# A conditioned attention and mixer block on one core: value products in one burst a unit, spread low halves in the MLP, attention's transfers in source order

## The chip, the core and the metric

The kernel runs on one core of a Trainium2 chip. The core has a matrix engine (TensorE, "PE" in the profile, with its weight loads shown apart as "PEld"), VectorE (DVE), ScalarE (ACT), GpSimdE (POOL) and SyncE (SP), which issues most of the transfers between memory (DRAM) and the on-chip buffers. Each engine works through its own queue in order and waits on semaphores for the others. TensorE writes its results to PSUM, which has eight banks; the other engines take them from there. The metric is the device time of one execution in microseconds (us).

## The reference

A sequence of 2048 rows of width 576 goes through attention over a sliding window of 256 rows, with 32 heads of 18, and then through a mixer block; both are modulated by a condition vector:

```
mod = silu(c) @ w_mod                      # sa, ca, ga, sb, cb, gb: six vectors of 576
h = layernorm(x) * (1 + ca) + sa
x = x + ga * (attention(h @ wqkv) @ wo)    # row i sees rows i-255 .. i
h = layernorm(x) * (1 + cb) + sb
x1 = h + shift(gelu(layernorm(h) @ w1)) @ w2       # quarters of the width shifted by +1, -1, +2, -2 rows
B  = x1 + gelu(layernorm(x1) @ w3) @ w4            # the MLP, hidden width 4608
x = x + gb * B
```

All data is float32. Large products are made in three parts: each operand is split into a high half (rounded to the engine's fast float32 form) and a low half (what is left), and high x high, high x low and low x high are added up.

## The kernel before

The kernel has three stages. The order of the work is written as a list of (time, function) pairs, which `play` sorts by time and runs; so a "time" in the code is a place in the order, not a duration. Under `manual_schedule` the engines named there keep that order; the queues of engines not named are ordered by the compiler's scheduler. In the attention stage and in the MLP, TensorE, VectorE, ScalarE and GpSimdE keep the written order, and SyncE's transfers are placed by the scheduler.

**Attention (phase_a).** Time counts units: 32 units, one for four heads of one group of 512 rows. For unit u, `pack(u)` at u-1.6 brings the unit's queries and keys by twelve transfers (L467, L469) into one of three buffers Q, K. Between u-1 and u, sixteen score products (L483) each go to VectorE for a masked maximum (L490). The maxima are transposed (L504), copied by ScalarE into a small tile `ms` (L509) and put by a transfer of ScalarE's queue (L510) into two more rows of the queries. Then, from u+0.38, the scores are made again, transposed, with the maximum already subtracted (L530, and L539 for the mask); ScalarE turns them into exponentials in tiles P (L549). A third of a unit has four heads in two P tiles; there are three thirds, b = 0, 1, 2. `av(b)` (L560) multiplies P with the values V: 32 columns of TensorE for each head. The results are copied to `avs` (L565), transposed (L571), divided and stored (L581). Between these, TensorE makes the queries, keys and values of the next group (L391), whose results pass POOL's split (L416) and are stored (L428 to L434), and later the output product with Wo (L785, stage s4). The raw weights wr of wqkv come through 'P' and 'r' buffers.

**Mixer (phase_b).** Products with w1 (L1016) and w2 (L1067). It isn't changed.

**MLP (phase_c).** Two blocks of 1024 rows, 18 units of 256 hidden columns each. `up` of a unit makes four wide results (L1276, 56 matmuls of 512 columns), which go through gelu on ScalarE to tiles g. From four g, POOL makes three combinations (L1249), so that the second product takes seven parts, m = 1, 2, 7, 4, 5, 6, 3 (a Strassen scheme). Each part is split: ScalarE writes the high half of a tile G (L1241), VectorE the low half (L1244). `down` of the unit before makes the seven narrow runs of twelve matmuls of 288 columns (L1322), into one of three pairs of PSUM banks; VectorE adds each pair of results to accA or accB (L1331). TensorE alternates: half of a wide result, a narrow run, and so on. In the first block the weights are also prepared: w3 and w4 are loaded (w4's rows are the tiles r, L1143), r is scaled by VectorE (L1164), combined by POOL (L1173), split by ScalarE and POOL (L1153, L1158; L1188, L1192), and the split weights are stored to w3d (L1160) and w4d (L1193). The second block only loads them again.

Of the kernel before, what the change touches and what calls it, by code (L numbers as in the profile page):

```python
# [18 lines left out]
D = 576  # L19
F = 4608  # L20
P = 128
# [32 lines left out]
class Kern:  # L54
# [134 lines left out]
    def phase_a(self):  # L189
# [9 lines left out]
        with ExitStack() as st:  # L199
# [91 lines left out]
            def w_load(c):  # L291
                def f():
                    raw = kp.tile([P, 1024], F32, tag="P", name=f"wr{c}", bufs=4)[:, 0:640] if c in (0, 4, 5, 1) else row(f"wr{c}")
# [178 lines left out]
            def scores(u):  # L472
# [34 lines left out]
                def ms():  # L507
                    ms = kp.tile([8, 512], F32R, tag="ms", name=f"ms{u}", bufs=1)
# [6 lines left out]
                return e + [(u + 0.01, neg), (u + 0.1, mt), (u + 0.115, ms)]  # L515
# [4 lines left out]
            def attend(u):  # L520
# [62 lines left out]
                for b in range(3):  # L583
# [3 lines left out]
                    e.append((u + self.o_x + (b + 1) / 3 + self.o_a, av(b)))  # L587
# [38 lines left out]

            def wo_begin():
                Wo["w"] = self.wv("Wo")
                Wo["ga"] = row("ga")[:, 0:D]
                nc.sync.dma_start(Wo["ga"], self.modd[2].to_broadcast([P, D]))  # L630

            def s4_begin():
                rows = gp.tile([P, 8, D], F32, tag="L", name="s4rows", bufs=1)
                self.s4row = lambda name: rows[:, next(cnt) % 8]
                self.sb, self.cb = (kp.tile([P, 1024], F32, tag="qe", name=n, bufs=2)[:, 0:D] for n in ("sb", "cb"))
                nc.sync.dma_start(self.sb, self.modd[3].to_broadcast([P, D]))
                nc.sync.dma_start(self.cb, self.modd[4].to_broadcast([P, D]))

            def wo_one(k, t):
                def f():  # L640
                    raw = row(f"wor{k}")[:, 0:D]
                    if k < KC:
                        nc.sync.dma_start(raw, self.wo[k * P:(k + 1) * P, :])
                        h, l = Wo["w"][:, k, :], Wo["w"][:, KC + k, :]
                    else:
                        self.load_dup(raw, self.wo[KC * P:, :])
                        h, l = Wo["w"][:, 2 * KC, :], Wo["w"][:, 2 * KC + 1, :]
                    Wo[k] = raw, h, l

                def scale():  # L650
                    raw = Wo[k][0]
                    nc.gpsimd.tensor_tensor(out=raw, in0=raw, in1=Wo["ga"], op=ALU.mult)

                def hi():
                    nc.scalar.copy(Wo[k][1], Wo[k][0])

                def lo():
                    raw, h, l = Wo[k]
                    nc.vector.tensor_tensor(out=l, in0=raw, in1=h.bitcast(F32), op=ALU.subtract)
                return [(t, f), (t + 0.2, scale), (t + 0.3, hi), (t + 0.36, lo)]  # L660
# [753 lines left out]
```

## Time and profile before

| | |
|---|---|
| median of 3 runs | 1755.18 us (1754.0 to 1764.7) |
| profiled execution | 1758.84 us |
| its span, first to last instruction | 1756.4 us |
| mean granted clock of TensorE | 0.990 |
| TensorE busy | 1684.1 us, 96% |
| VectorE busy | 1154.6 us, 66% |
| GpSimdE busy | 816.2 us, 46% |
| ScalarE busy | 711.8 us, 41% |

Times of one execution are read from the profile, whose own execution took 1758.84 us; the comparison of two kernels goes by the runs. A row of a group gives the line, the engine, the tiles written and read, the shape and the count; then busy time, the mean of one in ns, and the idle time before it with what ended most of it. A row of waits gives who waited for whom: us in all, how often, and the longest. A row of the timeline gives start and length in us, the engine and line, and in brackets the idle time before it. A row of a stretch gives its length, each engine's busy time, and then TensorE's granted clock, the share of the transfer engines, and GB/s. Attention fills the span up to some 690 us, the mixer up to some 860, the MLP the rest.

### The profile page before, as it was taken

The numbers are of one execution on the slowest core, as the hardware profiler recorded it, in microseconds if no ns is written. First come the engines' busy times: TensorE is split into PE (matmuls) and PEld (weight loads), VectorE is DVE, ScalarE is ACT, GpSimd is POOL, SyncE is SP. The second block draws the span as 40 slices with busy tenths as digits, with TensorE's granted clock in tenths as the row PEclk, the third lists the DMA queues.
The fourth block names the chain that finished last, engine by engine and source line by source line (L and its number), as shares of the span: only waits on it lengthen the run. The fifth ranks groups of instructions, "written<-read, shape, count | busy, mean of one in ns | idle before, by whom it ended". The sixth has DMA issues, their size and how long they took to land.

```text
span 1756.4 us, 30862 instructions
## 1 busy us (share of the span) xinstructions
PE 1684.1 (96%) x11100; PEld 1434.2 (82%) x11100; DVE 1154.6 (66%) x2543; ACT 711.8 (41%) x1310; POOL 816.2 (46%) x799
## 2 busy tenths in 40 slices
PE   8899999999999998999999999999999999999998
PEld 6767677777867776888988888888888999999997
DVE  3465565665667774767776666766676666666667
ACT  3254454554556556443344344434432222222321
POOL 7333141332235552134378777878865333333324
PEclk9999999999999999999999999999999999999999
DMA  6554445444356663545355555555555544444442
GB/s 196 175 164 144 117 140 143 129 132 128 98 151 189 198 197 124 180 126 169 129 207 177 171 203 206 183 176 201 202 212 195 161 149 153 147 150 158 154 142 74
DMA packets 161279, 283.33 MB, mean 161 GB/s; under 512 B 38500, under 2 KB 77412, under 8 KB 161128
## 3 DMA queue, kind: packets, MB, share of 16 engines
q1 hardware_dynamic: 158184, 275.54, 49.4%
q10 hardware_dynamic: 2944, 5.83, 1.2%
q8 instruction: 88, 1.44, 0.3%
q14 instruction: 63, 0.52, 0.1%
HBM read 168.86 MB, written 111.78 MB: 160 GB/s over the span
## 4 chain that ended last, share of the span: by engine, by line
PE 66%; POOL 9%; DVE 9%; DMA 7%; issue 4%; SPq 2%; ACT 2%; ACTq 0%; DVEq 0%; POOLq 0%
PE pall L1276 16%; PE pall L1322 16%; PE pall L391 8%; PE pall L560 4%; PE pall L530 4%; PE pall L483 4%; PE pall L1016 3%; PE pall L539 2%; PE pall L1067 2%; PE pall L785 2%; POOL g L1249 2%; POOL c L1173 2%; DMA r<-in_B_w_dram 2%; DVE accA L1331 1%; POOL W L1158 1%
## 5 line engine op out<-in xcount | busy, mean ns | idle before, releaser
L1276 PE MATMUL pall<-LNT,W 128*128 128x512 f32 x2016 | 501.1, 391 | 0.0
L1322 PE MATMUL pall<-W,G 128*128 128x288 f32 x3036 | 449.9, 296 | 20.8 <-DVE accB L1331 12.0
L1322 PEld LDWEIGHTS pall<-W,G 128*128 128x128 f32 x3036 | 431.5, 189 | 45.8 <-DVE accB L1331 16.3
L1276 PEld LDWEIGHTS pall<-LNT,W 128*128 128x128 f32 x2016 | 367.4, 189 | 60.5
L490 DVE CUSTOM_DVE_ANT_0 pall<-pall,mask 128x384 f32<-128x384 f32 (+2 forms) x512 | 271.8, 542 | 197.1 <-PE pall L483 194.4
L1331 DVE TENSOR_TENSOR accA<-pall,accA 128x576 f32<-128x576 f32 x336 | 248.4, 753 | 127.5 <-PE pall L1322 120.7
L1249 POOL TENSOR_TENSOR g<-g,g 128x512 f32<-128x512 f32 x140 | 191.1, 1365 | 257.1 <-ACT g L1280 240.6
L549 ACT ACTIVATE P<-pall 128x512 f32<-128x512 f32 (+2 forms) x384 | 216.5, 571 | 221.8 <-PE pall L539 199.9
L1244 DVE TENSOR_TENSOR G<-g,G 128x512 fp32r<-128x512 f32 x249 | 227.0, 928 | 50.0 <-ACT G L1241 49.8
L1241 ACT CAST G<-g 128x512 fp32r<-128x512 f32 x249 | 154.9, 622 | 239.9 <-POOL g L1249 236.4
L1280 ACT ACTIVATE g<-pall 128x512 f32<-128x512 f32 x144 | 85.8, 596 | 321.7 <-PE pall L1276 316.0
L483 PE MATMUL pall<-K,Q 108*128 108x384 f32 (+2 forms) x512 | 191.0, 380 | 10.1 <-DMA k1d<-qe 4.4
L530 PE MATMUL pall<-Q,K 110*128 110x384 f32 (+1 forms) x704 | 156.4, 296 | 10.0 <-ACT P L549 7.3
L391 PE MATMUL pall<-hT,Wc 128*128 128x512 f32 x504 | 160.2, 416 | 1.3 <-ACT V L454 1.0
L530 PEld LDWEIGHTS pall<-Q,K 110*128 110x128 f32 x704 | 123.7, 191 | 35.9 <-ACT P L549 16.1
L1331 DVE TENSOR_TENSOR accB<-pall,accB 128x576 f32<-128x576 f32 x134 | 97.8, 750 | 65.8 <-PE pall L1322 64.8
L416 POOL CAST qe<-qe 128x512 fp32r<-128x512 f32 x36 | 22.7, 630 | 253.2 <-ACT qe L412 233.1
L539 PE MATMUL pall<-maskb,identb 128*128 128x256 bf16 (+1 forms) x640 | 121.0, 255 | 0.0
L483 PEld LDWEIGHTS pall<-K,Q 108*128 108x128 f32 x512 | 97.5, 193 | 22.3 <-issue 11.4
L560 PE MATMUL pall<-P,V 128*32 128x384 f32 (+2 forms) x1408 | 100.5, 396 | 0.0
L391 PEld LDWEIGHTS pall<-hT,Wc 128*128 128x128 f32 x504 | 86.9, 194 | 13.7 <-issue 4.1
L391 PE MATMUL pall<-Wv,hT 128*128 128x288 f32 x448 | 84.1, 311 | 2.6 <-POOL Wv L334 2.4
(648 smaller groups left out, 2067.7 us busy)
## 6 DMA issues: line engine op xcount, KB each, us to landing
w4d<-W SPq DMA_DIRECT2D x55, 576.0 KB
W<-w4d SPq DMA_DIRECT2D x55, 576.0 KB
w3d<-W SPq DMA_DIRECT2D x36, 640.0 KB
W<-w3d SPq DMA_DIRECT2D x36, 640.0 KB
K<-k0d SPq DMA_DIRECT2D x96, 108.0 KB
r<-in_B_w_dram SPq DMA_DIRECT2D x36, 288.0 KB
Q<-q0d SPq DMA_DIRECT2D x128, 72.0 KB
K<-k1d SPq DMA_DIRECT2D x48, 108.0 KB
```

What stands on the lines that cost most here:

```text
L391: nc.tensor.matmul(pm, pl()[i][0], pl()[i][1], start=(i == 0), stop=(i == 13))
L483: nc.tensor.matmul(sc[:, lo:], q[0:2 * R3, h, i * P:(i + 1) * P], k[0:2 * R3, h // 2, i * P + lo:(i + 3) * P], start=True, stop=True)
L490: nc.vector.tensor_tensor_reduce(out=sc[:, lo:], in0=sc[:, lo:], in1=mask[:, lo:], scale=1.0, scalar=-3e38, op0=ALU.add, op1=ALU.max, accu ...
L530: nc.tensor.matmul(x[:, p0 * P:(p0 + w) * P], k[0:2 * R3 + 2, h // 2, (kb + 2) * P:(kb + 3) * P], q[0:2 * R3 + 2, h, q0 * P:(q0 + w) * P], ...
L539: nc.tensor.matmul(x[:, p0 * P:(p0 + w) * P], self.identb, m, start=False, stop=(n == len(ms) - 1))
L549: nc.scalar.activation(pt[:, c0:c1, h % 2, :], x[:, c0 * P:c1 * P].rearrange("p (a b) -> p a b", b=P), AF.Exp, scale=SCALE)
L560: nc.tensor.matmul(abox[0][32 * h:32 * h + 32, q0 * P:(q0 + w) * P], v[:, hh * VA:hh * VA + 32], Pt[b, h // 2][:, p0:p0 + w, h % 2, :], st ...
L1244: nc.vector.tensor_tensor(out=sp[m][:, 1], in0=src(), in1=sp[m][:, 0].bitcast(F32), op=sub)
L1249: nc.gpsimd.tensor_tensor(out=g[o] if o in g else gt(o), in0=g[a], in1=g[b], op=op)
L1276: nc.tensor.matmul(box["p"], box["l"][i][1], box["l"][i][0], start=(i == 0), stop=(i == 13))
L1322: nc.tensor.matmul(po, a, b, start=(n == 0), stop=(n == len(seq) - 1))
L1331: nc.vector.tensor_tensor(out=acc2[m, i], in0=po, in1=acc2[m, i], op=ALU.add)
```

## The change

It changes the order of the work and some buffers; every product, split and transfer is still made. Its parts:

1. The three `av(b)` of a unit stand directly behind one another at the end of the unit. Seven P tiles instead of four; `ms` uses the buffer of `avs`; a reserved scratch space is made smaller, which gives the room. The transposes of the maxima come 0.03 unit later.
2. In phase_a SyncE is under the written order as well. Some places move: the raw weights wr6 earlier, `pack(1)` from -0.6 to -1.5, the loads of Wo earlier and its splits farther behind them, sb and cb later, x rows of s4 earlier.
3. In the MLP the splits of G are spread over the unit, one low half behind each narrow run; two of POOL's combinations write to other tiles; scaling and combining of r come about 0.15 unit later; the stores to w3d and w4d are events of their own (`keep`), 0.3 unit behind the high halves.
4. The last unit of the first block runs its parts in the common order, with its final sums and stores to match.

```
-                            Pt[b, h // 2] = kp.tile([P, 4, 2, P], F32, tag="P", name=f"P{u}_{b}_{h}", bufs=4)
+                            Pt[b, h // 2] = kp.tile([P, 4, 2, P], F32, tag="P", name=f"P{u}_{b}_{h}", bufs=7)
...
-                    ms = kp.tile([8, 512], F32R, tag="ms", name=f"ms{u}", bufs=1)
+                    ms = kp.tile([8, 512], F32R, tag="avs", name=f"ms{u}", bufs=1)
...
-                return e + [(u + 0.01, neg), (u + 0.1, mt), (u + 0.115, ms)]
+                return e + [(u + 0.01, neg), (u + 0.13, mt), (u + 0.15, ms)]
...
-                    e.append((u + self.o_x + (b + 1) / 3 + self.o_a, av(b)))
+                    e.append((u + self.o_x + 1 + self.o_a - 0.001 * (2 - b), av(b)))
...
-            wt = {0: -8.975, 4: -8.974, 5: -8.973, 1: -8.972, 6: -2.7, 2: -1.9, 7: -1.5, 3: -1.2, 8: -0.9}
+            wt = {0: -8.975, 4: -8.974, 5: -8.973, 1: -8.972, 6: -7.45, 2: -1.9, 7: -1.5, 3: -1.2, 8: -0.9}
...
-                ev.append((u - self.o_p if u else -7.3, pack(u)))
+                ev.append((u - self.o_p if u > 1 else (-7.3, -1.5)[u], pack(u)))
...
-            ev += [(w1 - 1.25, wo_begin), (w1 + 0.03, s4_begin)]
+            ev += [(w1 - 1.7, wo_ga), (w1 - 1.15, wo_begin), (w1 + 0.03, s4_begin), (w1 + 0.4, s4_mod)]
             for k in range(KC + 1):
-                ev += wo_one(k, w1 - 1.2 + 0.12 * k)
+                ev += wo_one(k, w1 - 1.65 + 0.1 * k)
...
-            with self.tc.manual_schedule(engines={mybir.EngineType.PE, mybir.EngineType.DVE, mybir.EngineType.Activation, mybir.EngineType.Pool}):
+            with self.tc.manual_schedule(engines={mybir.EngineType.SP, mybir.EngineType.PE, mybir.EngineType.DVE, mybir.EngineType.Activation, mybir.EngineType.Pool}):
...
-                nc.sync.dma_start(self.w3d[fg][j], w.bitcast(F32))
-            return f, hi, lo
+
+            def keep():
+                nc.sync.dma_start(self.w3d[fg][j], w3[j].bitcast(F32))
+            return f, hi, lo, keep
...
-        e = [] if blk else [(0.42, load), (0.8, scale(0)), (0.84, scale(1))] + [(t, comb(n)) for n, t in enumerate((0.87, 0.91, 0.96, 1.02))]
+        e = [] if blk else [(0.42, load), (0.95, scale(0)), (0.98, scale(1))] + [(t, comb(n)) for n, t in enumerate((1.0, 1.03, 1.07, 1.11))]
...
-            e += [(t, f)] if blk else [(t, f), (t + 0.001, hi), (t + 0.035, lo)]
+            e += [(t, f)] if blk else [(t, f), (t + 0.001, hi), (t + 0.035, lo), (t + 0.3, keep)]
...
-            def after(n, t):
+            def after(n):
                 src = lambda k: lambda: g[k]
-                if n < 2 or plain:
-                    return split((1, 2, 7, 4)[n], src(n), t + 0.03)
+                if plain:
+                    return split((1, 2, 7, 4)[n], src(n), t0 + 0.28 + 0.25 * n)
+                if n < 2:
+                    return split((1, 2)[n], src(n), t0 + 0.63 + 0.125 * n, 0.085)
                 if n == 2:
-                    return [(t + 0.045, comb(4, 0, 2, sub))] + split(7, src(4), t + 0.13)
-                e = split(4, src(3), t + 0.03) + [(t + d, comb(*x)) for d, x in ((0.045, (2, 2, 3, add)), (0.1, (0, 2, 0, sub)), (0.155, (1, 1, 0, sub)))]
-                return e + [x for m, k, d in ((5, 2, 0.105), (6, 0, 0.16), (3, 1, 0.215)) for x in split(m, src(k), t + d)]
+                    return [(t0 + 0.795, comb(4, 0, 2, sub))] + split(7, src(4), t0 + 1.0, 0.09)
+                e = [(t0 + t, comb(*x)) for t, x in ((1.045, (2, 2, 3, add)), (1.235, (3, 2, 0, sub)), (1.36, (2, 1, 3, sub)))]
+                return e + [x for m, k, a, b in ((4, 3, 1.1, 1.215), (5, 2, 1.25, 1.34), (6, 3, 1.38, 1.465), (3, 2, 1.5, 1.59)) for x in split(m, src(k), t0 + a, b - a)]
...
-            ms = (2, 4, 5, 3) if plain else (1, 2, 7, 6, 5, 4, 3) if last else (1, 2, 7, 4, 5, 6, 3)
+            ms = (2, 4, 5, 3) if plain else (1, 2, 7, 4, 5, 6, 3)
...
-    nc = _bacc.Bacc("TRN2", target_bir_lowering=False, num_devices=1)
+    nc = _bacc.Bacc("TRN2", target_bir_lowering=False, num_devices=1, dynamic_dma_scratch_size=1024)
```

How the order of three engines moves. First TensorE, in the middle of attention. Before, one third of a unit's value products (two P tiles with two blocks of rows each) stands between score products, and the other two thirds stand some 35 rows ahead and behind:

```order
L483 MATMUL pall<-K_174,Q_171 128x384
L560 MATMUL pall<-P_0_0_3435,V_163 32x384 x2
L560 MATMUL pall<-P_0_2_3465,V_163 32x384 x2
L560 MATMUL pall<-P_0_0_3435,V_166 32x128 x2
L560 MATMUL pall<-P_0_2_3465,V_166 32x128 x2
L483 MATMUL pall<-K_174,Q_171 128x384
L530 MATMUL pall<-Q_170,K_173 128x384
```

Now all three thirds of a unit, in its six P tiles, follow each other:

```order
L560 MATMUL pall<-P_0_0_3419,V_163 32x384 x2
L560 MATMUL pall<-P_0_2_3465,V_163 32x384 x2
L560 MATMUL pall<-P_0_0_3419,V_166 32x128 x2
L560 MATMUL pall<-P_0_2_3465,V_166 32x128 x2
L560 MATMUL pall<-P_1_0_3499,V_164 32x384 x2
L560 MATMUL pall<-P_1_2_3522,V_164 32x384 x2
L560 MATMUL pall<-P_1_0_3499,V_161 32x128 x2
L560 MATMUL pall<-P_1_2_3522,V_161 32x128 x2
L560 MATMUL pall<-P_2_0_3555,V_162 32x256 x2
L560 MATMUL pall<-P_2_2_3583,V_162 32x256 x2
L560 MATMUL pall<-P_2_0_3555,V_165 32x256 x2
L560 MATMUL pall<-P_2_2_3583,V_165 32x256 x2
```

One burst of 48 matmuls took the place of three of 16.

Then SyncE's queue near the end of the first group's projections. Before, the loads of raw weights wr3 and wr8 stand ahead of the first of unit 1's twelve transfers to Q1 and K1:

```order
L117 DMA wr7_570<-in_A_wqkv_dram 64x128
L299 DMA wr3_600<-in_A_wqkv_dram 128x4x128
L116 DMA wr3_600<-in_A_wqkv_dram 64x128
L117 DMA wr3_600<-in_A_wqkv_dram 64x128
L299 DMA wr8_621<-in_A_wqkv_dram 128x4x128
L116 DMA wr8_621<-in_A_wqkv_dram 64x128
L117 DMA wr8_621<-in_A_wqkv_dram 64x128
L467 DMA Q1_170<-q0d0_137 18x2x512
L469 DMA K1_173<-k0d0_145 18x2x512
```

Now unit 1's transfers follow wr7, and wr3 comes behind the last of them:

```order
L117 DMA wr7_570<-in_A_wqkv_dram 64x128
L467 DMA Q1_170<-q0d0_137 18x2x512
L469 DMA K1_173<-k0d0_145 18x2x512
L467 DMA Q1_170<-q1d0_138 18x2x512
L469 DMA K1_173<-k0d0_145 18x2x512
```

Six loads moved from ahead of them to behind them.

Last VectorE in a unit of the MLP's first block. Before (L1331 an eviction to accA or accB, L1244 a low half of G, L1164 the scaling of r), two pairs of low halves stand between evictions, and a scaling stands behind an eviction:

```order
L1331 TENSOR_TENSOR accA<-pall,accA 128x576 x2
L1164 TENSOR_TENSOR r_0_11363<-r_0_11363,gb 128x576
L1331 TENSOR_TENSOR accA<-pall,accA 128x576 x2
L1164 TENSOR_TENSOR r_1_11365<-r_1_11365,gb 128x576
L1244 TENSOR_TENSOR G_7_11473<-g_7_4_11445,G_7_11473 128x512
L1331 TENSOR_TENSOR accB<-pall,accB 128x576 x2
L1244 TENSOR_TENSOR G_7_11494<-g_7_3_11491,G_7_11494 128x512
L1244 TENSOR_TENSOR G_7_11513<-g_7_2_11443,G_7_11513 128x512
L1331 TENSOR_TENSOR accB<-pall,accB 128x576 x2
L1244 TENSOR_TENSOR G_7_11523<-g_7_0_11318,G_7_11523 128x512
L1244 TENSOR_TENSOR G_7_11542<-g_7_1_11388,G_7_11542 128x512
```

Now (the same lines are L1338, L1249 and L1167):

```order
L1249 TENSOR_TENSOR G_7_11440<-g_7_1_11381,G_7_11440 128x512
L1167 TENSOR_TENSOR r_0_11353<-r_0_11353,gb 128x576
L1167 TENSOR_TENSOR r_1_11355<-r_1_11355,gb 128x576
L1338 TENSOR_TENSOR accB<-pall,accB 128x576 x2
L1249 TENSOR_TENSOR G_7_11476<-g_7_4_11444,G_7_11476 128x512
L1338 TENSOR_TENSOR accB<-pall,accB 128x576 x2
L1249 TENSOR_TENSOR G_7_11508<-g_7_3_11488,G_7_11508 128x512
L1338 TENSOR_TENSOR accA<-pall,accA 128x576 x2
L1249 TENSOR_TENSOR G_7_11540<-g_7_2_11442,G_7_11540 128x512
L1338 TENSOR_TENSOR accA<-pall,accA 128x576 x2
L1249 TENSOR_TENSOR G_7_11580<-g_7_3_11488,G_7_11580 128x512
```

Each low half stands behind one pair of evictions, and both scalings stand together in the stretch that has no narrow run.

More of the change, by code (lines that the diff above doesn't have):

```diff
@@ L625, in phase_a, with wo_ga @@
             cnt = itertools.count()
+            def wo_ga():
+                Wo["ga"] = row("ga")[:, 0:D]
+                nc.sync.dma_start(Wo["ga"], self.modd[2].to_broadcast([P, D]))
             def wo_begin():
                 Wo["w"] = self.wv("Wo")
-                Wo["ga"] = row("ga")[:, 0:D]
-                nc.sync.dma_start(Wo["ga"], self.modd[2].to_broadcast([P, D]))
             def s4_begin():
@@ L744, in load_x @@
         def load_x():
-            box["x"] = self.s4row(f"xr{t}")
+            box["x"] = self.s4row(f"xr{t}") if t else self.row("xr0")[:, 0:D]
             nc.sync.dma_start(box["x"], self.x[t * P:(t + 1) * P, :])
@@ L1282, in up @@
                 ev += [(t, part(0, 7)), (t + 0.125, part(7, 14))]
-                ev += [(t + 0.255, gelu)] + after(n, t + 0.25)
+                ev += [(t + 0.255, gelu)] + after(n)
             return ev
```

55 lines of the change are left out of this document (27 added, 28 removed).

## The prediction

> **What bounds the kernel now.** I read the page first, for the engine shares and the chain that ended last, and then the stages by time, since the shares are averages.
>
> ```profile
> PE 1684.1 (96%) x11100; PEld 1434.2 (82%) x11100; DVE 1154.6 (66%) x2543; ACT 711.8 (41%) x1310; POOL 816.2 (46%) x799
> PE 66%; POOL 9%; DVE 9%; DMA 7%; issue 4%; SPq 2%; ACT 2%; ACTq 0%; DVEq 0%; POOLq 0%
> ```
>
> PE is busy for 96% of the span and is two thirds of the chain. The change adds and removes no matmul, so it can gain only where PE waits, where PE is slow at a switch between kinds of work, or where its clock is halved. The MLP shows its floor itself. The next view counts the wide matmuls (L1276, 56 a unit) in two stretches, the first from the MLP's second unit to the end of its first block, the second in the second block; the next two rows are all engines in the same stretches.
>
> ```profile
> 873.60:1352.00 478.40, 266.16 (x1065) 194.71 (x1065) 0.99 0.56 193
> 1375.80:1709.00 333.20, 194.03 (x785) 142.08 (x784) 1.00 0.48 152
> 873.60:1352.00 478.40, 461.91 (x2661) 414.20 (x2661) 331.39 (x436) 184.84 (x344) 365.12 (x308) 0.99 0.56 193
> 1375.80:1709.00 333.20, 333.20 (x1961) 302.58 (x1960) 225.03 (x294) 93.05 (x154) 114.68 (x87) 1.00 0.48 152
> ```
>
> 1065 / 56 is 19 units of 25.2 us; 785 / 56 is 14 units of 23.8 us with PE busy all of the time (333.20 of 333.20). So 23.8 us is PE's own price of a unit, the second block has nothing to give, and the first stands 478.4 - 19 x 23.8 = 26.2 us above it. The waits in that stretch, of PE, DVE, POOL and SP in turn, tell why.
>
> ```profile
> PE pall L1322 <- DVE accB L1331: 12.0, 10, 3.2
> PE pall L1322 <- DVE accA L1331: 3.0, 2, 1.6
> DVE G L1244 <- ACT G L1241: 49.4, 20, 3.9
> DVE r L1164 <- DMA r<-in_B_w_dram: 25.0, 13, 4.3
> POOL c L1173 <- DVE r L1164: 54.7, 28, 4.7
> SPq L1193 <- POOL W L1192: 161.0, 66, 7.0
> ```
>
> Read from the bottom it is one chain: SP stands 161 us at w4d stores that wait for POOL's low halves; the next unit's w4 rows (r) are therefore issued late; DVE stands at the scaling of r; POOL's combinations of r, and the combinations of g queued behind them, come late; ACT's high halves of G come late; DVE stands at the low halves (L1244), which are queued ahead of evictions, and PE waits for PSUM.
>
> **The value products (three bursts a unit become one).** Attention is the other stage. The loads of weights, then the matmuls, around one of today's bursts:
>
> ```profile
> 305.51 0.16 PEld L560 LDWEIGHTS pall<-P,V 128*32 128x32 f32 x8 [0.37 <-issue]
> 306.51 0.19 PEld L483 LDWEIGHTS pall<-K,Q 108*128 108x128 f32 x1 [0.20 <-issue]
> ...
> 301.63 0.34 PE L483 MATMUL pall<-K,Q 108*128 108x384 f32 x1
> 301.80 0.39 PE L530 MATMUL pall<-Q,K 110*128 110x384 f32 x2
> ...
> 303.42 1.09 PE L391 MATMUL pall<-hT,Wc 128*128 128x512 f32 x4
> 304.35 0.40 PE L530 MATMUL pall<-Q,K 110*128 110x384 f32 x2
> ...
> 304.95 0.63 PE L391 MATMUL pall<-hT,Wc 128*128 128x512 f32 x2
> 305.51 1.07 PE L560 MATMUL pall<-P,V 128*32 128x384 f32 x16
> 306.51 0.44 PE L483 MATMUL pall<-K,Q 108*128 108x384 f32 x1
> 306.79 0.40 PE L530 MATMUL pall<-Q,K 110*128 110x384 f32 x2
> ```
>
> Going in: four L391 take 303.42 to 304.35, 0.23 us each, so the two at 304.95 should hand over at 305.41; the burst starts at 305.51, 0.10 late. Coming out: the load of L483 starts with its matmul (306.51), not ahead of it, after the load side idled 0.20; about half of that the last narrow group (128 columns) needs anyway, so 0.10. Then L530 follows L483 by 0.28 us instead of 0.17 (301.63 to 301.80): 0.11 more. In and out together: 0.31 us. There are 32 units and two of three ins and outs go: 64 x 0.31 = **-20 us**. Ends: only the 0.10, -6 us; the load side's whole idle, 0.37 + 0.20, -36 us. I take 0.31, which is what the matmul rows show.
> [...]
>
> What the burst needs in return: six P tiles of a unit are held to its end, so the next unit's first exponentials take the seventh and then those that the burst's first products free; the burst stands ahead of them in PE's order, so no circle. The avs buffer now also carries ms; ms is written at u+0.15, the avs copy at u+0.59, and eight microseconds between them cover the ms transfer. The transposes of the maxima move from u+0.10 to u+0.13, 0.03 x 18.7 us (a unit, 310.39 to 329.11 between two L504 rows) = 0.6 us nearer to the products that wait for the ms transfer. And scores and exponentials stand closer together where a burst lay between. These costs are late waits of a kind that exists:
>
> ```profile
> 310.39 0.40 PE L504 MATMUL pall<-identr,mr 128*8 128x128 f32 x4
> 329.11 0.41 PE L504 MATMUL pall<-identr,mr 128*8 128x128 f32 x4 [0.16 <-DVE mr L497]
> PE pall L530 <- ACT P L549: 7.3, 7, 2.2
> PE pall L530 <- DMA Q<-ms: 2.6, 4, 1.0
> ```
>
> I take 6 us more for both together (they are 9.9 now); ends 0 and 15 (each unit 0.5 us). **+6 us.**
>
> **The transfers in source order.** Two stalls of PE on transfers:
>
> ```profile
> 57.76 0.60 SPq L117 DMA_DIRECT2D wr<-in_A_wqkv_dram  x1
> 58.40 0.51 SPq L467 DMA_DIRECT2D Q<-q0d  x1
> 62.78 0.27 SPq L469 DMA_DIRECT2D K<-k1d  x1
> 66.79 0.33 PE L483 MATMUL pall<-K,Q 108*128 108x128 f32 x1 [4.39 <-DMA k1d<-qe]
> 487.00 6.58 SPq L879 DMA_DIRECT2D W14r<-in_B_w_dram  x9
> 493.68 0.49 SPq L467 DMA_DIRECT2D Q<-q0d  x1
> 506.05 0.42 PE L483 MATMUL pall<-K,Q 108*128 108x384 f32 x1 [3.39 <-DMA sb<-modd]
> 50.00:100.00 50.00, 44.19 (x291) 35.01 (x291) 30.13 (x121) 19.70 (x41) 15.54 (x23) 0.97 0.55 170
> 200.00:250.00 50.00, 46.56 (x362) 35.83 (x362) 33.04 (x111) 26.05 (x48) 15.56 (x22) 0.97 0.42 118
> 500.00:550.00 50.00, 45.03 (x386) 35.21 (x388) 31.89 (x114) 24.62 (x46) 18.00 (x22) 0.97 0.66 180
> ```
>
> At 66.79 PE waited for unit 1's K, whose twelve transfers (58.40 to 62.78) stood behind six transfers of later weights (wr3, wr8, some 4.5 us at the 0.5 to 0.6 us that each issue row shows). In the new order they stand ahead of these. At 506.05 the scores waited for transfers that stood behind nine small loads of w1 (487.00, 6.58 us of issue, the unit's first transfer at 493.68); the new order puts these behind them. 4.4 + 3.4 = 7.8; I take **-7 us**. In both stretches PE's clock is 0.97, 0.03 x 50 = 1.5 us; with the stall this goes too: **-3 us**. Ends for both terms: 0 and -14 (with the wait near 206 and its clock).
> [...] The row from 200 to 250 has 0.97 as well, though no idle of PE there exceeds the 2.2 us shown above, so shorter stalls cost clock here too, and I leave that side open.
> Other moves of this part (Wo, sb and cb, x rows, the first weights) lie under PE work with microseconds of cover; I cost them at nothing. If one loses its cover, its transfer shows as a stall of some 3 us, as at 506.05.
>
> **The MLP.** DVE's two groups there:
>
> ```profile
> L1331 DVE TENSOR_TENSOR accA<-pall,accA 128x576 f32<-128x576 f32 x336 | 248.4, 753 | 127.5 <-PE pall L1322 120.7
> L1244 DVE TENSOR_TENSOR G<-g,G 128x512 fp32r<-128x512 f32 x249 | 227.0, 928 | 50.0 <-ACT G L1241 49.8
> ```
>
> Four of seven low halves stood in pairs between evictions; now each stands behind one narrow run. A run's step is 23.8 / 8 = 3.0 us, and DVE has for it two evictions (0.75 us each) and one low half (0.93): 2.4. The stores leave 0.3 unit later, so SP is free for r, and the scaling comes 0.15 unit later still. What is late next is POOL: two of its combinations of g now write over tiles that DVE's low halves read, so POOL waits for DVE twice a unit. POOL is busy 365.12 / 19 = 19.2 us of a unit of 23.8, so 4.6 us a unit are there for it. Of the 26.2 us I take **-21**, leaving first and last units of the block their waits. Ends: -8 (the accB waits fall by two thirds) and -26. The tail (plain unit) keeps its order: 0.
>
> **Sum.** -20 + 6 - 7 - 3 - 21 = -45 us. The profiled execution took 1758.84 us (span 1756.4), which gives 1713.8; the median of the runs shown is 1755.18, 3.7 below it, and **1710 us** is that less 45.
>
> **Rivals.**
> *The switch is cheap*: PE's matmul records are modelled at their ends, and only the 0.10 us of the entry is real. Then that term is -6: 1724. For it: the load side idles between narrow groups as well; against it: 0.28 against 0.17 behind the burst.
> *POOL becomes the bound of the MLP's first block*: its two new waits on DVE, each up to a step of 3.0 us, use up the 4.6 us to spare, and a unit stays at 25.2. Then the MLP gives nothing: 1755 - 24 = 1731. For it: POOL's 76%, and 54.7 us at DVE already; against it: DVE's low halves are then evenly spread and early.
> *SP in source order falls behind (slower)*: SP can no longer pass a store that waits. The rows:
>
> ```profile
> SPq L802 <- POOL s4rows L801: 36.0, 10, 7.0
> SPq L432 <- POOL qe L416: 20.8, 6, 6.6
> ```
>
> The twelve transfers of a unit follow at u-1.6 and are wanted at u-0.97, 0.63 x 18.7 = 11.8 us later; their issue took 4.4 us (58.40 to 62.78) and the last landed within 4 us (66.79), so 3.4 us are to spare. A store that holds SP for 7 us ahead of them in every unit leaves PE 3.6 us waiting, 32 x 3.6 = 115 us; with the -45 that is 1825. It decides from 3.4 + 45 / 32 = 4.8 us a unit. Against it: the stores stood near these places already, and such waits are 16 in 32 units.
> *It does nothing*: the orders of PE, SP and DVE above show that it does.
>
> **How the numbers follow.** The forecast 0.70 (1695 to 1724), cheap switch 0.10, POOL bound 0.10, SP behind 0.05, small gains cancelled by new waits (about 1750) 0.05. The range reaches over the first three: **1692 to 1733**. About 1%, 17.5 us, is what a measurement of this kernel can tell from no change: below 1737.6 is faster, 0.88; same 0.07; slower 0.05.
>
> **What would show it.** L560's "issue" idle on the load side about 20 us lower and its bursts x48 in a row; the MLP's first block at 24 us a unit, DVE's wait for r and PE's for accB all but gone, SP's wait at the w4d stores a small part of 161; no idle of 3 us near 62 and 503. I am wrong if attention keeps its length: then PE was not its bound there, or POOL, ACT or SP gave the gain back.

## The result, and the profile after

The changed kernel takes **1739.25 us** (median of 4 runs, 1731.9 to 1744.0) against 1756.26 us for the kernel before in the same comparison: a ratio of 0.9891, 95% interval 0.9843 to 0.9939. The gain is 17 us where 45 were forecast, and the time lies above the range of 1692 to 1733. The profiled execution took 1739.16 us (span 1737.4).

First the page of the changed kernel: busy time of the engines, and the engines' shares of the chain that ended last. PE's share of the chain rose from 66% to 81%.

```profile
PE 1665.6 (96%) x11100; PEld 1439.1 (83%) x11100; DVE 1172.6 (67%) x2543; ACT 700.9 (40%) x1310; POOL 812.6 (47%) x799
PE 81%; DMA 6%; DVE 5%; POOL 3%; ACT 2%; issue 1%; SPq 1%; ACTq 0%; POOLq 0%; DVEq 0%
```

**The MLP** did what was forecast. In the changed kernel, all engines from the MLP's second unit to the end of its first block, 19 units:

```profile
876.80:1332.30 455.50, 452.89 (x2662) 410.83 (x2660) 367.30 (x436) 177.90 (x342) 367.15 (x308) 1.00 0.59 203
```

The stretch fell from 478.4 to 455.5 us, by 22.9; 455.5 is 19 x 23.8 + 3.3, and PE is busy 452.89 of it. The waits of DVE, POOL and SP in it:

```profile
DVE G L1249 <- ACT G L1246: 1.9, 1, 1.9
POOL g L1254 <- DVE G L1249: 34.9, 21, 2.0
POOL c L1176 <- DVE r L1167: 31.3, 16, 2.7
SPq L1144 <- POOL W L1195: 62.8, 24, 7.6
SPq L1139 <- POOL W L1195: 61.4, 7, 8.8
SPq L1198 <- POOL W L1195: 49.2, 28, 10.8
```

DVE no longer stands at its low halves (49.4 us before) nor at r, and PE's waits for accA and accB are gone. The new wait of POOL for DVE exists, 34.9 us over 19 units, 1.8 us a unit of the 4.6 that were to spare. SP waits 49 us at the w4d stores (161 before), but in all it stands for POOL's splits about as long as before: with 93.9 us at the w3d stores 267 us, against 161 + 117.5 = 279. Now 124 of them are at the loads of the next unit's raw weights (L1139, L1144), so the weights are asked for as soon as POOL has done with their buffers. Which of the part's edits did it, the later stores, the later scaling or the spread splits, no run separates.

**Attention and the start** gave nothing back. All engines before and after the first L504 row (the first transposes of the maxima), up to the first row of w1's use; first the kernel before, then the changed one (columns: window, length, PE busy, weight loads, DVE, ACT, POOL, granted clock, DMA share, GB/s):

```profile
0.00:68.30 68.30, 56.13 (x261) 42.72 (x262) 26.82 (x96) 19.59 (x38) 43.95 (x61) 0.94 0.68 197
68.30:692.40 624.10, 597.25 (x4786) 463.94 (x4784) 391.60 (x1332) 331.34 (x610) 213.41 (x252) 0.99 0.50 145
```

```profile
0.00:72.40 72.40, 58.98 (x263) 43.61 (x264) 26.99 (x97) 19.58 (x38) 43.88 (x61) 0.93 0.65 178
72.40:697.10 624.70, 584.99 (x4786) 471.20 (x4783) 384.97 (x1330) 330.24 (x610) 213.01 (x252) 0.98 0.52 146
```

PE is busy 12.3 us less in attention, and the stretch is as long as before: what the bursts saved stands there as waiting, at a lower clock. The start is 4.1 us longer. The largest waits of PE in attention, changed kernel (waiter, whom it waited for, us in all, times, longest):

```profile
PE pall L530 <- ACT P L549: 12.4, 15, 3.6
PE pall L530 <- DMA Q<-ms: 4.1, 4, 1.7
PE pall L483 <- DMA xnd<-s4rows: 4.0, 1, 4.0
PE pall L483 <- DMA k0d<-qe: 2.9, 1, 2.9
```

The wait of 4.0 us shows how SP comes into it. SP's rows ahead of it and PE's row, changed kernel:

```profile
629.64 0.44 SPq L984 DMA_DIRECT2D xn<-xnd  x1
635.15 0.32 SPq L803 DMA_DIRECT2D hbd<-s4rows  x1
635.52 2.35 SPq L984 DMA_DIRECT2D xn<-xnd  x5
...
638.44 0.30 SPq L467 DMA_DIRECT2D Q<-q0d  x1
...
647.83 0.27 SPq L469 DMA_DIRECT2D K<-k1d  x1
653.24 0.41 PE L483 MATMUL pall<-K,Q 108*128 108x384 f32 x1 [4.02 <-DMA xnd<-s4rows]
```

SP stood from 630 to 635 at the store of hbd, whose data POOL had not written (4.7 us); behind it in the source stood five loads of xn for the next stage and a store of xp, and only then the unit's twelve transfers of Q and K. Their issue took 9.4 us, where that of the twelve at 58.40 in the kernel before took 4.4; the last was issued at 647.83. PE's row names another transfer, the one nearest to the end of its wait; the late ones are those of Q and K, 5.4 us after whose last issue PE goes on. The largest of the 15 waits for ACT's exponentials, 3.60 us at 583.81, has a transfer in its chain too: up to 582.41 ACT stood 4.94 us at a normalization of the third stage's rows (L158), for what the trace names the transfer xp<-s4rows.

### The profile page after: what moved, and what is told of

It reads as the page before. It is cut to its first block, busy times and chain, and to the rows that moved or that the text cites. A ratio compares the mean times of both kernels' runs of the same rounds, so it can differ in the third digit from the quotient of the medians.

```text
span 1737.4 us, 30750 instructions
## 1 busy us (share of the span) xinstructions
PE 1665.6 (96%) x11100; PEld 1439.1 (83%) x11100; DVE 1172.6 (67%) x2543; ACT 700.9 (40%) x1310; POOL 812.6 (47%) x799
## 4 chain that ended last, share of the span: by engine, by line
PE 81%; DMA 6%; DVE 5%; POOL 3%; ACT 2%; issue 1%; SPq 1%; ACTq 0%; POOLq 0%; DVEq 0%
PE pall L1283 26%; PE pall L1329 22%; PE pall L391 8%; PE pall L560 4%; PE pall L530 4%; PE pall L483 4%; PE pall L1017 3%; PE pall L539 3%; PE pall L1068 2%; PE pall L786 2%; DVE pall L490 1%; DMA Q<-ms 1%; DMA wm<-in_w_mod_dram 1%; PE pall L276 1%; PE pall L571 1%
## 5 line engine op out<-in xcount | busy, mean ns | idle before, releaser
L1329 PE MATMUL pall<-W,G 128*128 128x288 f32 x3036 | 443.4, 295 | 5.7 <-DVE G L1249 3.6
L1338 DVE TENSOR_TENSOR accA<-pall,accA 128x576 f32<-128x576 f32 x336 | 254.2, 757 | 127.3 <-PE pall L1329 115.2
L1254 POOL TENSOR_TENSOR g<-g,g 128x512 f32<-128x512 f32 x140 | 183.9, 1314 | 293.5 <-DVE G L1249 151.1
L1246 ACT CAST G<-g 128x512 fp32r<-128x512 f32 x249 | 151.0, 620 | 282.0 <-POOL g L1254 280.3
L1249 DVE TENSOR_TENSOR G<-g,G 128x512 fp32r<-128x512 f32 x249 | 241.5, 971 | 4.1 <-ACT G L1246 4.1
L483 PE MATMUL pall<-K,Q 108*128 108x384 f32 (+2 forms) x512 | 188.4, 379 | 13.5 <-DMA xnd<-s4rows 4.0
L530 PE MATMUL pall<-Q,K 110*128 110x384 f32 (+1 forms) x704 | 156.8, 297 | 16.7 <-ACT P L549 12.4
L391 PE MATMUL pall<-hT,Wc 128*128 128x512 f32 x504 | 159.2, 415 | 3.4 <-ACT V L454 1.9
L1338 DVE TENSOR_TENSOR accB<-pall,accB 128x576 f32<-128x576 f32 x134 | 101.4, 757 | 89.8 <-PE pall L1329 87.7
L530 PEld LDWEIGHTS pall<-Q,K 110*128 110x128 f32 x704 | 125.1, 192 | 39.1 <-ACT P L549 20.9
L483 PEld LDWEIGHTS pall<-K,Q 108*128 108x128 f32 x512 | 97.5, 195 | 21.4 <-issue 8.8
L391 PEld LDWEIGHTS pall<-hT,Wc 128*128 128x128 f32 x504 | 86.1, 192 | 17.3 <-issue 3.9
L391 PE MATMUL pall<-Wv,hT 128*128 128x288 f32 x448 | 85.0, 313 | 3.5 <-POOL Wv L334 2.4
L560 PE MATMUL pall<-P,V 128*32 128x384 f32 (+2 forms) x1408 | 86.9, 394 | 0.0
```

Source lines behind the costliest of these rows:

```text
L391: nc.tensor.matmul(pm, pl()[i][0], pl()[i][1], start=(i == 0), stop=(i == 13))
L483: nc.tensor.matmul(sc[:, lo:], q[0:2 * R3, h, i * P:(i + 1) * P], k[0:2 * R3, h // 2, i * P + lo:(i + 3) * P], start=True, stop=True)
L530: nc.tensor.matmul(x[:, p0 * P:(p0 + w) * P], k[0:2 * R3 + 2, h // 2, (kb + 2) * P:(kb + 3) * P], q[0:2 * R3 + 2, h, q0 * P:(q0 + w) * P], ...
L560: nc.tensor.matmul(abox[0][32 * h:32 * h + 32, q0 * P:(q0 + w) * P], v[:, hh * VA:hh * VA + 32], Pt[b, h // 2][:, p0:p0 + w, h % 2, :], st ...
L1249: nc.vector.tensor_tensor(out=sp[m][:, 1], in0=src(), in1=sp[m][:, 0].bitcast(F32), op=sub)
L1254: nc.gpsimd.tensor_tensor(out=g[o] if o in g else gt(o), in0=g[a], in1=g[b], op=op)
```

## The experiments

All twelve runs below are compared with the kernel before on their own chip; "ratio" is that comparison, with its 95% interval. Where a length of attention is given, it is that between the first L504 row and the first row of w1's use in the profiled execution.

### First four: the parts apart

**MLP alone.** Kernel before with the edits of `w3d`, `w4d`, `scale`, `comb`, `after(n)` and the tail's order, nothing else.

> Kernel before with the MLP part of the change alone. The two traces show 22.9 us less from the first MLP unit to the start of its second block, so if that part stands by itself this kernel takes 1755 - 23 = 1732 us (1727 to 1737), attention as before (624 us between the first L504 row and the first row of w1's use). If the MLP's gain needs the source order of SP in attention (its first weights come earlier), it is under 15 us: above 1740.

1735.98 us, ratio 0.9889 (0.9874 to 0.9903): -19.5 us, attention 624.7. The MLP's term stands by itself.

**The burst alone.** Kernel before with:

```diff
-tag="P", ..., bufs=4      +tag="P", ..., bufs=7
-tag="ms"                  +tag="avs"
-(u + 0.1, mt), (u + 0.115, ms)      +(u + 0.13, mt), (u + 0.15, ms)
-u + self.o_x + (b + 1) / 3 + self.o_a, av(b)
+u + self.o_x + 1 + self.o_a - 0.001 * (2 - b), av(b)
...
```

The smaller scratch space and one smaller buffer, which make the room, are in it too.

> Kernel before with the value products in one burst (the seven P buffers, ms in the avs buffers, its later times) and nothing else. Theory A, the source order of SP gave attention's gain back: the burst alone keeps -20 + 6 = -14 us, 1741 (1735 to 1746), PE's idle in attention up by under 7 us. Theory B, the burst itself gives it back, since scores, exponentials and the maxima's transfer come closer together: within 5 us of before, 1750 to 1758, with the waits of L530 for ACT P and for DMA Q<-ms at 16 us as in the changed kernel (9.9 before).

1752.75 us, ratio 0.9974 (0.9956 to 0.9991): about -4 us. Neither theory as written: theory B's time, with waits of its own size (L530 for ACT P and for Q<-ms 12.5 us together). Attention in the profile:

```profile
68.80:684.20 615.40, 581.26 (x4785) 469.72 (x4783) 389.40 (x1330) 330.87 (x610) 214.26 (x252) 0.99 0.50 147
```

PE is busy 16.0 us less than the kernel before (597.25), idle 7.3 us more (615.40 - 581.26 = 34.1 against 26.8). These 8.7 us are those of two profiled executions, 1750.06 against 1758.84 us; the medians of the comparison differ by 2.7.

**Source order and moved loads, three bursts.** Kernel before with the transfers' part alone (with it some splits of Wo and the first products of wr6 move a little).

> Kernel before with the transfers' part alone: SP in source order in attention, the moved loads of x, wr6, Wo, sb, cb and pack(1); value products in three bursts, MLP as before. The prediction's own term: -10 us, 1745. Theory A: it costs +12 to +18 us, 1767 to 1773 (4 of them before the first L504 row). Theory B: the order by itself costs only the 4 us of the start, 1757 to 1761.

1758.48 us, ratio 1.0019 (1.0003 to 1.0036): +3 us. The forecast's -10 is refuted; which of its two halves costs is not yet told by this run.

**SP free.** Changed kernel with one edit:

```diff
-manual_schedule(engines={EngineType.SP, EngineType.PE, EngineType.DVE, EngineType.Activation, EngineType.Pool})
+manual_schedule(engines={EngineType.PE, EngineType.DVE, EngineType.Activation, EngineType.Pool})
```

> Changed kernel, SP's instructions in attention ordered by the scheduler as before and not by the source; all else as changed (also the moved loads). Theory A (source order of SP gave the gain back): 12 us or more below the changed kernel, under 1728. Theory B (burst gave it back): within 5 us of the changed kernel's 1739, or some us above it.

1721.56 us, ratio 0.9797 (0.9764 to 0.9829): 17 us below the changed kernel. Theory A's prediction. The same two stretches:

```profile
0.00:64.50 64.50, 56.46 (x263) 42.82 (x264) 26.48 (x97) 19.58 (x38) 43.95 (x61) 0.95 0.69 200
64.50:678.80 614.30, 579.06 (x4785) 467.36 (x4782) 386.25 (x1330) 330.83 (x610) 212.80 (x252) 0.99 0.51 148
```

7.9 us came back at the start and 10.4 in attention. Of these 18.3, some 9 are clock: adding up half the length of each half-clock stretch (one in which the trace has the clock at 0.50), over the whole trace 20.4 us are lost in the changed kernel and 11.5 here (mean clocks of 0.989 and 0.994).

### Next: where the source order costs, and what the burst is worth without it

**SP free up to play time -1.6 only** (in source order from there; four matmuls of a V item also run ahead of fourteen L391, since the play is cut in two).

```diff
+with manual_schedule(engines=four):               rest = play(ev, -1.6)
+with manual_schedule(engines=four | {EngineType.SP}):  play(rest)
```

> Changed kernel with SP ordered by the scheduler up to shortly before the first unit (play time -1.6), and by the source from there. The kernel with SP free throughout took 1721.6 us, 17.7 less than the changed one; its profile shows 7.9 of them before the first L504 row (72.4 against 64.5) and 10.4 between that row and w1's first use. If the two are independent: first L504 row at 64 to 65, attention 624 to 626, 1731 (1727 to 1735). Rival: the stalls within attention follow from the start (transfers that come late once stay late); then this kernel takes 1722 to 1726 with attention at 616 or less.

1735.20 us, ratio 0.9892 (0.986 to 0.9924): no gain by the ratio. Its two stretches:

```profile
0.00:68.50 68.50, 58.95 (x264) 44.67 (x265) 30.27 (x97) 19.59 (x38) 44.20 (x61) 0.90 0.67 195
68.50:694.80 626.30, 586.78 (x4785) 473.32 (x4782) 386.73 (x1330) 330.60 (x610) 213.60 (x252) 0.98 0.52 145
```

Attention stays at 626 although the start is 3.9 us shorter, so the rival falls as far as this reaches: its stalls are no echo of the start. The start came back by half only (68.5, not 64.5); some 3 of the 4 us that are missing are clock (0.90 over 68.5 us against 0.95 over 64.5). Why the clock was halved more often here stays open.

**Maxima at their old times, SP free** (`mt` and `ms` back at u + 0.1 and u + 0.115).

> Changed kernel with SP free throughout and the transposes of the maxima and the ms copy back at their old times in the unit (0.1 and 0.115 in place of 0.13 and 0.15). In the SP-free kernel PE waits 11.4 us for DMA Q<-ms ahead of L530. If that wait comes from the later times, 0.035 x 19 us = 0.7 us a unit come back: the wait falls to 2 to 4 us and the time to 1711 to 1715. If it comes from ms sharing the avs buffer, or from other transfers in the DMA queues, it stays at 9 us or more and the time at 1719 to 1724.

1717.85 us, ratio 0.9792 (0.976 to 0.9824), by the ratio the same as without the edit, and between the two expectations. The wait for Q<-ms fell from 11.4 to 8.8 only:

```profile
PE pall L530 <- DMA Q<-ms: 8.8, 7, 2.7
...
PE pall L504 <- DVE mr L497: 3.6, 7, 1.0
```

PE now stands at the transposes instead, for DVE's maxima (1.2 us with the later times). So the later times cause at most 2.6 of the 11.4 us, and the time doesn't show these.

**Three bursts, SP free** (the line of `av(b)` undone).

> Changed kernel with SP free throughout and the value products in three bursts a unit again (seven P buffers and the later ms kept). The prediction's price of a switch, 0.31 us for each in and out: 64 x 0.31 = 20 us more switching, less the 12 us or so of new waits that the burst alone showed: 1721.6 + 8 to 1721.6 + 20, so 1730 to 1742, L560's bursts 97 instead of 33. If the price is only the entry's 0.10: at most 1728.

1724.06 us, ratio 0.9829 (0.9789 to 0.9868). The burst is worth 3 to 6 us here (medians, ratios), and the two intervals overlap, so by this pair alone it may be nothing. The time fits the second expectation (at most 1728), but not by its reason, as PE's busy time below shows. Its attention, and then PE's two largest waits in it:

```profile
64.80:681.10 616.30, 593.99 (x4786) 463.14 (x4783) 386.85 (x1330) 330.85 (x610) 213.32 (x252) 0.99 0.51 148
```

```profile
PE pall L530 <- ACT P L549: 7.0, 7, 2.1
PE pall L530 <- DMA Q<-ms: 3.8, 4, 1.7
```

The same waits with one burst and SP free:

```profile
PE pall L530 <- DMA Q<-ms: 11.4, 8, 2.2
PE pall L530 <- ACT P L549: 8.0, 14, 2.3
```

PE is busy 593.99 - 579.06 = 14.9 us less with one burst, and idle 12.9 us more (35.2 against 22.3). The switches' price is real (not only the entry's 0.10), and most of it comes back as waiting.

### Last: each half of the transfers, and the chain over the maxima

**Moved loads alone**, SP free, three bursts, MLP as before.

> Kernel before with the moved loads alone (x, wr6, Wo, sb, cb, pack(1)), SP ordered by the scheduler as before: the kernel of e_order without the source order. If the loads' new places took the stalls near 62 and 503 away (4.4 + 3.4 us and the half-clock of both, 1.7 us each), 1755 - 11 = 1744 us (1740 to 1748), which makes the source order of SP cost e_order's 1758.5 - 1744 = 14 us with three bursts too. If the moved loads help only where the value products stand in one burst: 1752 to 1757.

1742.66 us, ratio 0.9921 (0.989 to 0.9952): -14 us, the first expectation. The largest waits of L530 and L483 in its attention:

```profile
PE pall L530 <- ACT P L549: 5.9, 7, 2.4
PE pall L530 <- DMA Q<-ms: 4.1, 4, 1.3
PE pall L483 <- DMA k0d<-qe: 2.1, 1, 2.1
```

And in that of the kernel with SP in source order on top (the run above with ratio 1.0019):

```profile
PE pall L530 <- ACT P L549: 11.1, 10, 3.4
PE pall L483 <- DMA od<-o: 3.9, 2, 2.0
PE pall L483 <- DMA xp<-s4rows: 1.5, 1, 1.5
```

So the two stalls of 4.4 and 3.4 us went with the loads' places, and on top of these the source order costs 1.0019 - 0.9921, 17 us, with three bursts as well as with one. No run has the source order without the moved loads.

**Stores later, SP in source order.** Changed kernel with:

```diff
-(0.12, store)             +(0.25 if g else 0.12, store)
-on: nc.sync.dma_start(od)   at t + 0.165      +put_o at t + 0.365
-mod: nc.sync.dma_start(hbd) at 1.14           +put_h at 1.34
-ln2: nc.sync.dma_start(xnd) at 1.62           +put_n at 1.78
```

> Changed kernel, SP in source order, with four kinds of stores played later, behind work of SP that does not wait: od 0.2 of a unit later, q and k halves of the groups after the first 0.13 later, the two stores of the third stage's rows (hbd, xnd) 0.2 and 0.16 later. If SP standing at a store whose data is not there holds back the transfers behind it, attention falls from 624.7 towards the 614.3 that it takes with SP free: 1728 to 1734. If the cause is another (which transfer shares a queue with which, or the loads' places), it stays at 622 to 627 and the time at 1736 to 1742.

1731.01 us, ratio 0.9849 (0.9817 to 0.9881), and attention at 615.7:

```profile
0.00:70.20 70.20, 57.66 (x264) 42.54 (x265) 26.69 (x97) 19.60 (x38) 43.92 (x61) 0.95 0.69 185
70.20:685.90 615.70, 578.70 (x4786) 467.28 (x4782) 384.40 (x1330) 330.21 (x610) 213.04 (x252) 0.99 0.53 148
```

9.0 of the 10.4 us that the source order costs in attention come back when SP meets these stores later, still in source order (8 us by the medians of the whole): where these stores stand in the order is the cause there. 6.3 of the 9.0 are PE's busy time, at a clock of 0.99 against 0.98, and 2.7 its idle time. That it is by the transfers behind the stores is read from the rows at 653.24 and argued for the rest. SP's standing by itself costs nothing: it stands 49.2 us at the od stores here, 51.2 in the changed kernel and 76.4 with SP free. What is left against SP free lies mostly at the start (70.2 against 64.5).

**More room for the chain over the maxima**, SP free, maxima at their old times:

```diff
-o_p, o_x, o_a, g_w = 1.6, 0.38, 0.18, 0.05
+o_p, o_x, o_a, g_w = 1.56, 0.42, 0.14, 0.05
```

> Changed kernel with SP free, the maxima's transposes and ms at their old times (0.1, 0.115), and the second products and exponentials of a unit 0.04 of a unit later against the scores (0.42 for 0.38, the burst kept at its place). PE waits there 8.8 us for DMA Q<-ms and 7.0 for ACT P when they stand at 0.38 (1717.9 us). If these waits are latency of the chain from the last score to the first product (7.4 us there, 8.4 with three bursts), 0.75 us more room a unit takes the ms wait to 2 to 4 us: 1711 to 1714. If the room is lost elsewhere (exponentials then closer to the burst, K/Q buffers free later), 1717 or more.

1727.97 us, ratio 0.9844 (0.9809 to 0.9879): slower than without the edit. The waits of PE in attention:

```profile
PE pall L530 <- ACT P L549: 6.2, 14, 1.0
PE pall L504 <- DVE mr L497: 4.8, 6, 1.8
PE pall L483 <- DMA k0d<-qe: 4.0, 1, 4.0
PE pall L483 <- DMA od<-o: 2.9, 3, 1.7
PE pall L786 <- DVE oT L773: 2.8, 2, 1.6
```

The wait for Q<-ms is down to 1.1 us, and others stand in its place; attention is 621.2 us. The rival's time holds (1717 or more): the room given to one chain cost more elsewhere. Since the edit also brings a unit's queries and keys 0.04 of a unit later (1.56 for 1.6), the 4.0 us for k0d may come from that.

**No product waits for the maxima**, one burst and three.

```diff
-nc.scalar.dma_start(q[2 * R3:2 * R3 + 2, :, :].bitcast(F32), ms.bitcast(F32))
+nc.scalar.dma_start(self.msd[u % 3], ms.bitcast(F32))
...
-AF.Exp, scale=SCALE
+AF.Exp, scale=0.05 * SCALE
```

These two kernels leave out the shift by the maxima, and their exponentials are of scores scaled down.

> Changed kernel with SP free and one burst a unit, where the maxima are still computed, transposed and copied, but their transfer goes to a buffer in device memory that nobody reads: the products run without the maxima (exponentials of scores scaled down, unshifted), so this leaves out the shift and no product waits for DMA Q<-ms. Beside the same edit with three bursts. If the chain over the maxima eats the burst's gain, this kernel is 11 us below 1721.6, at 1709 to 1713, and 10 to 15 us below its three-burst sibling. If other waits would take its place anyway (exponentials, K/Q transfers, V copies), it is at 1716 or more and within 6 us of the sibling.

> The same edit (maxima's transfer to a buffer nobody reads, exponentials unshifted: the shift is left out) on the kernel with SP free and three bursts a unit. It waits 3.8 us for DMA Q<-ms with the shift: 1724 - 4 = 1720 (1717 to 1724) by either theory; the difference to the one-burst sibling decides.

1713.95 us, ratio 0.9733 (0.971 to 0.9756), with one burst; 1719.02, ratio 0.9783 (0.9751 to 0.9815), with three. Between the two theories: the one-burst kernel is 5 us faster by the medians and 9 by the ratios. Attention with one burst, then with three:

```profile
66.60:672.30 605.70, 575.41 (x4786) 466.29 (x4783) 387.16 (x1330) 331.17 (x610) 213.43 (x252) 0.99 0.53 151
```

```profile
64.40:678.70 614.30, 593.34 (x4786) 463.25 (x4782) 388.74 (x1330) 332.03 (x610) 213.83 (x252) 0.99 0.52 148
```

PE is busy 17.9 us less with one burst and idle 9.3 us more (30.3 against 21.0). With the maxima's wait it was 12.9 us more: that chain accounts for 3.6 of the 12.9 us. The largest wait that is left is for ACT's exponentials, 10.5 us with one burst and 6.6 with three. Of the 17.9 us, 3.4 are clock: the trace of the three-burst run has two more stretches of 3.4 us at the halved clock in attention.

The version that beats both kernels is the changed one with SP free: 1721.56 us, and 1717.85 with the maxima at their old times, which is not told apart from it; nor is the one with SP free and three bursts (1724.06).

## Why the prediction was wrong, point by point

| term | forecast | measured | by |
|---|---|---|---|
| MLP | -21 | -19.5 | MLP alone |
| transfers: loads moved | -10 together | -14 | moved loads alone |
| transfers: SP in source order | in the -10 | +17 | source order, against moved loads alone; SP free, against the changed kernel |
| value products in one burst | -20 | -15 to -16 | PE's busy time, first two pairs |
| new waits of the burst | +6 | +7 to +13 | PE's idle time, first two pairs |
| sum | -45 | -17 | the changed kernel |

By these two pairs (the burst alone against the kernel before; one burst against three with SP free), burst and waits together are -8.7 (16.0 against 7.3) and -2.0 (14.9 against 12.9), and the terms add up to -18 to -25; with the 3 to 6 us that the times show for the burst, to -20 to -23. The ratio 0.9891 is 19 us, the medians 17.

**The step that failed is "the transfers in source order".** The two stalls were read rightly, and they went (with the moved loads alone the half-clock stretch of 3.4 us near 507 went too, but one at 64.5 stayed, and the clock up to the first L504 row is 0.94 as before). But the forecast put their cause into SP's order, and took the source order and the moved loads for one term with one sign. The runs separate them: the moved loads, with the scheduler free to order SP, gave 14 us (8 to 19 by the interval), no less than both together were to give, and the source order took 17. The prediction named this as a rival (SP falls behind, a store holds SP ahead of the twelve transfers) and priced it wrongly in form: it priced a stand in every unit, which cancels the gain from 4.8 us a unit on, as though it came everywhere or nowhere. It came at a few places and at the start. At 653.24 it was a store, and PE waited 4.0 us. At 404.13 PE waited 2.9 us, and there SP was held not by a store: it stood 5.5 us at the last of the twelve transfers itself (issued at 401.16), for what the trace names the load of wm. After both, PE's clock was halved for 3.4 us. "Other moves of this part lie under PE work; I cost them at nothing" failed in both directions: the loads' new places gave 3 us at the start (first L504 row at 65.1 with the moved loads alone, 68.3 before), and the source order lost 8 there (72.4 against 64.5 with SP free; with three bursts 4.5, 69.6 against 65.1). The waits of PE before 72.4, changed kernel, and then before 64.5 with SP free:

```profile
PE pall L276 <- DMA wm<-in_w_mod_dram: 3.1, 1, 3.1
PE pall L483 <- DMA K<-k1d: 2.6, 1, 2.6
```

```profile
PE pall L276 <- DMA wm<-in_w_mod_dram: 0.9, 1, 0.9
```

The two are 2.2 + 2.6 us, and the start has three half-clock stretches against two (0.93 over 72.4 us, 0.95 over 64.5), 1.7 us more: 6.5 of the 7.9 us.

**The value products.** The switches were mis-sized by a quarter: 14.9 and 16.0 us over 64 ins and outs are 0.23 and 0.25 us, not 0.31 (0.21 to 0.25 over all three pairs, with the half-clock stretches taken out). The prediction read its price from one burst, and it took 0.10 us of the load side's 0.20 us of idle behind it as a price of leaving; without that it is 0.21. The changed kernel's one burst shows the same idle inside it:

```profile
313.45 2.80 PE L560 MATMUL pall<-P,V 128*32 128x384 f32 x48
313.45 0.16 PEld L560 LDWEIGHTS pall<-P,V 128*32 128x32 f32 x8 [0.36 <-issue]
313.80 0.13 PEld L560 LDWEIGHTS pall<-P,V 128*32 128x32 f32 x4 [0.19 <-issue]
314.12 0.35 PEld L560 LDWEIGHTS pall<-P,V 128*32 128x32 f32 x12 [0.19 <-issue]
314.66 0.13 PEld L560 LDWEIGHTS pall<-P,V 128*32 128x32 f32 x4 [0.19 <-issue]
314.98 0.78 PEld L560 LDWEIGHTS pall<-P,V 128*32 128x32 f32 x20 [0.19 <-issue]
```

So this idle of 0.19 us belongs to the narrow groups themselves: it stands inside the first two thirds, twice in each, as it does in the kernel before (there at 305.86 and 306.18), and at the two places where bursts were joined, behind the 16th and the 32nd load, there is none. Over attention the "issue" idle of L560's loads fell from 45.0 to 35.0 us, by 10 where 20 were to be seen.

**The new waits** were the other mis-sized part: +6 was taken and +15 was the upper end; 7 and 13 were measured. The bursts that stood between the last score and the first product had been cover for the maxima's transfer and for ACT's exponentials: this is read from the waits, and only the maxima's part, 3.6 us, was taken away by itself. Together, burst and waits leave 3 to 6 us of the 14 that were forecast. This remains so with SP free, and the source order costs 17 us with three bursts too; so it did not eat the burst's gain, and the two losses add.

**The MLP** was right in size, and the waits that it named went: DVE's for r and for G, PE's for accB. POOL's part of the chain eased only (31.3 us at DVE's r against 54.7), and SP still stands for POOL, at other places. Cheap switch and POOL bound, the two rivals that reached the upper end of the range, did not occur. The outcome is a mix of the two rivals that had 0.05 each, SP behind, in a weak form, and gains cancelled by new waits, with the MLP's gain kept. At 1739.25 us it lies above the 1737.6 below which the prediction, with 0.88, called the kernel faster.

"I am wrong if attention keeps its length: then PE was not its bound there, or POOL, ACT or SP gave the gain back": it kept its length. The source order of SP gave some 10 us back there, and PE's new waits, those for the maxima and the exponentials among them, the rest.

## What to carry to other kernels

In a queue whose order is fixed by hand, a store that waits for its data holds the transfers behind it (4.7 us at 630 here). Before fixing it, look for each wait of that queue (here for POOL's and DVE's results) at what stands behind it, and play stores late and apart from their computation. This gave 9 us in attention; in the MLP it was one edit of several behind the 20. A change with two edits of one purpose, "loads moved" and "order fixed", needs two terms. And work that is taken out from between a producer's last and its consumer's first instruction was cover (PE's idle rose by 7.3 and 12.9 us here): price the chain that it covered, with its transfer, before counting its time as gained.

## What the runs showed of the hardware that was not expected

A short stall of PE can cost more than itself: here 1.72 us of waiting were followed by 3.41 us at half the clock. The row at which PE had waited 1.72 us in the changed kernel; then the engines in the stretches behind the 2.88 us wait at 404.13 and behind this one, and in the stretch that follows the first:

```profile
468.40 0.47 PE L530 MATMUL pall<-Q,K 110*128 110x384 f32 x2 [1.72 <-DMA Q<-ms]
```

```profile
405.00:408.40 3.40, 3.40 (x18) 3.19 (x17) 1.37 (x6) 1.25 (x3) 0.00 (x0) 0.50 0.01 5
470.00:473.30 3.30, 3.30 (x26) 1.19 (x28) 0.50 (x2) 0.29 (x1) 1.71 (x2) 0.50 0.61 149
408.50:411.90 3.40, 3.40 (x24) 3.13 (x24) 2.30 (x8) 2.14 (x5) 0.00 (x0) 1.00 0.16 44
```

Each time the clock is 0.50 for 3.41 us and then whole again: 1.7 us lost behind a stall of 1.7 to 2.9 us. Not each such stall is followed by one (in the changed kernel's MLP, PE's waits of 1.93 us at 1314.74 and of 2.12 us at 1716.96 have none: the clock is 1.00 in the 10.0 and in the 5.5 us behind them), and the runs of one kernel differ by it: the four of the changed kernel have mean clocks of 0.986 to 0.994, and the slowest and the fastest of them have these two. Span times mean clock, an estimate of the span at the whole clock from these runs, is 1717.8 to 1719.7 us for the four: nearly all of their spread of 12 us is clock. By the same estimate the SP-free kernels take 1705.3 to 1709.8 us with one burst and 1708.4 to 1709.2 with three, so that the burst is worth next to nothing there, and the source order costs some 10 us of its 17 without the clock.
